# Windowed attention and a gated feed-forward on one core: 2 key tiles for every query tile from batch 2 on, output stores issued by ScalarE, another order of the first requests

## The chip, the core and the metric

The kernel runs on one core of a Trainium2 chip. The metric is the device time of one execution in microseconds (us), the median of several runs. TensorE (PE in the profile) multiplies; VectorE (DVE), ScalarE (ACT) and GpSimd (POOL) do elementwise work; SyncE (SP) only issues DMAs. ACT and POOL issue DMAs too.

## What is computed

The reference, cut to what matters:

```python
# q, k, v: (4, 8, 768, 64); n_sink = 4, window = 128; scale = 1/8
keep = (key < n_sink) | ((query - key >= 0) & (query - key < window))
a = softmax(where(keep, scale * q @ k.T, -1e9))
x = (a @ v)                       # -> (3072, 512), heads side by side
out = (relu(x @ w_gate) * (x @ w_val)) @ w_out     # d_ff = 1536
```

A query sees itself, the 127 keys ahead of it, and the first four keys of the sequence (the sinks).

## The kernel before

**Units and slots.** A unit is a pair of heads of one batch: 16 units, unit i is batch i // 4, pair i % 4. The order of all work is written out by hand in 96 slots. Slots 24b to 24b+23 hold the first feed-forward product of batch b: `chunk(b, g, m)` makes one tile of 128 hidden columns for half of the batch's 768 rows (g), four accumulating matmuls with w_gate and four with w_val (L362), a relu by ACT (L377) and a product by DVE (L379). After the chunk come the attention steps that `plan` lists for the slot, then from slot 24 on three matmuls of the second feed-forward product (`ffn2`, L404). Twelve of these make one output tile; ACT copies it out of PSUM (L408) and SP stores it (L409). `prep` lists what is issued ahead of a slot's chunk: loads, casts, transposes, copies.

**Attention of a unit** is spread over slots of the batch before. `Sg` computes scores for groups of key tiles (keys on partitions, L290; two matmuls a segment, one per head, on 64 rows each), exponentials by ACT (L298) and a product with a 0/1 mask by DVE (L300). `W` multiplies the exponentials by the values, 65 columns at a time (the 65th is ones, for the sum; L325), and DVE divides (L330, L331). Key tiles are 128 keys at the rows of `VROW`: even tiles start at 0, 244, 496, 748, odd tiles hold the four sinks and 124 keys. Because of this a query tile sometimes needs three key tiles. `SEG` lists the score segments of each group, `QSEG` which pieces each of the seven query tiles adds up: 10 segments and 16 pieces a head.

**Keys and queries on time.** For batches 2 and 3 the loads (`load_rows`, L161), the casts by POOL (`cast_rows`, L166), a store to DRAM in bfloat16 (`to_dram`, L171) and a transposing DMA into KQ (`turn`, L175) prepare a unit; POOL then copies the odd key tiles and the sinks in KQ (`odd_tiles`, L185 and L181), in the slot before the unit's first scores. Values are loaded by SP (`load_v`, L131) into one buffer `vf` and cast by POOL into `vn` (`cast_v`, L134): batch 2 loads in slots 23 to 29 and casts in 28 to 34, batch 3 loads in 44 to 50 and casts in 47 to 53.

**The way of the result.** For batches 2 and 3 a unit's normalised result goes by two SP stores to DRAM (`x_to_dram`, L151) in the slot after its `W`, and comes back by a transposing DMA two slots later into xT (`x_turn`, L155). Units 8 to 11 (batch 2) have their `W` in slots 35, 37, 39 and 41; the chunks of batch 2 begin at slot 48 and read all four quarters of xT.

**SP's queue is in order.** SP issues loads, stores and transposes as they are listed; an issue that must wait holds back all behind it. POOL's weight loads (L190) are in order with POOL's casts.

**Front.** Batch 0 is loaded in halves (`load_half`, L113: half c is pair c % 4, first or second 384 rows) and cast by POOL (`cast_half`, L118). SP requests the keys of halves 0 to 3, three value tiles, then halves 4 and 5; halves 6 and 7 and the other values wait for a write by DVE (L449). POOL's order is: cast of half 4, cast of half 5, weights of tiles 4 and 5; in slot 1 the cast of half 6, weights of tiles 6 and 7, the cast of half 7. Slot 6 holds the second half of W of units 0 and 1, which needs the other values.

Of the kernel before, what the change touches and what calls it, by code (L numbers as in the profile page):

```python
# [10 lines left out]
BF16 = mybir.dt.bfloat16  # L11
Alu = mybir.AluOpType
# [9 lines left out]
def kernel(  # L22
# [12 lines left out]
    nc = tc.nc  # L35
    B, H, S, D = q.shape
# [20 lines left out]
    KQ = [const.tile([128, 2 * S + 408], BF16, name=f"KQ{i}") for i in range(NT)]  # L57
    qT = [x[:, 0:S] for x in KQ]
    kE = [x[:, S:2 * S + 408] for x in KQ]
# [13 lines left out]
    msk = const.tile([128, 3, 512], BF16, name="msk")  # L73
    mb = const.tile([128, 2, 512], BF16, name="mb")
# [21 lines left out]
            [(4, 2, 128), (5, 2, 272)], [(5, 2, 396), (6, 2, 252), (4, 2, 416)]]  # L96

# [34 lines left out]

    def cast_v(b, j, rows=128, copy=nc.gpsimd.tensor_copy):
        copy(vn[b % 2][0:rows, j, :, 0:64], vf[0:rows, j, :, :])  # L134
# [10 lines left out]
    xd = [nc.dram_tensor(f"xd{i}", (1008, 128), BF16, kind="Internal").ap() for i in range(ND, B * NP)]  # L145

    def x_to_dram(u):

        x, d = xn[u.i % 2], xd[u.i - ND]
        for t, r0, n, i in ((0, 0, 128, 4), (1, 128, 124, 3)):  # L150
            nc.sync.dma_start(out=d[r0:r0 + 252 * i, :].rearrange("(i r) c -> r i c", r=252)[0:n, :, :],  # L151
                              in_=x[0:n, t:t + 2 * i - 1:2, :])

    def x_turn(u):
        nc.sync.dma_start(out=xT[u.b % 2][:, u.p, :], in_=xd[u.i - ND][8:8 + S, :], transpose=True)  # L155
        for x in range(2):
            ready[u.b, u.p, x] = True
# [78 lines left out]

    rot = [0]
# [41 lines left out]
    def Sg(u, s, ps=None):  # L279
        t, bias = u.i % NT, u.b == 0 and s in (0, 3)  # L280
        g, b0, n, segs = SEG[s]
        ps = ps or pair()
        at = [ps[h][:] if isinstance(ps, list) else ps[:, h, :] for h in range(2)]
        if bias:
            for h in range(2):
                nc.tensor.matmul(out=at[h][:, b0:n], lhsT=ident[:], rhs=mb[:, g, b0:n], start=True, stop=False,
                                 skip_group_check=True)
        for x0, q0, c0, c1 in segs:
            for h in range(2):
                nc.tensor.matmul(out=at[h][:, c0:c1], lhsT=kE[t][64 * h:64 * h + 64, x0:x0 + 128],  # L290
                                 rhs=qT[t][64 * h:64 * h + 64, q0:q0 + c1 - c0], start=not bias, stop=True,
                                 skip_group_check=True)
        x = ee[u.i % NE][:, g, :, b0:n]
        if isinstance(ps, list):
            for h in range(2):
                nc.scalar.activation(x[:, h, :], at[h][:, b0:n], Act.Exp, bias=0.0, scale=scale)
        else:
            nc.scalar.activation(x, ps[:, :, b0:n], Act.Exp, bias=0.0, scale=scale)  # L298
        if not bias:
            nc.vector.tensor_tensor(x, x, msk[:, g, b0:n].unsqueeze(1).to_broadcast([128, 2, n - b0]), op=Alu.mult)  # L300
# [9 lines left out]
    def W(u, part=None, bank=None):  # L310

        tiles = PART[part][0]
# [8 lines left out]
        for h in range(2):  # L321
            for t in tiles:
                c = 65 * (t - tiles[0])
                for i, (j, g, c0) in enumerate(QSEG[t]):
                    nc.tensor.matmul(out=at[h][:, c:c + 65], lhsT=ee[u.i % NE][:, g, h, c0:c0 + 128],  # L325
                                     rhs=vn[u.b % 2][:, j, 2 * u.p + h, 0:65],
                                     start=c == 0 and i == 0 and (bank is None or h == 0),
                                     stop=t == tiles[-1] and i == len(QSEG[t]) - 1, skip_group_check=True)
# [57 lines left out]
    def ffn2(b, t, m):  # L386
# [19 lines left out]
        if m == FM - 1:  # L406
            ot = outpool.tile([128, d_model], F32, name="ot")
            nc.scalar.copy(ot[:], op)  # L408
            nc.sync.dma_start(out=out[b * S + t * 128:b * S + (t + 1) * 128, :], in_=ot[:])  # L409

    with tc.manual_schedule():
# [6 lines left out]
        for c in (4, 5):  # L418
            load_half(c)
# [17 lines left out]
        for j in range(3):  # L437
            cast_v(0, j, copy=dve if j == 2 else nc.gpsimd.tensor_copy)
        load_w(2, 4)
        cast_half(4)  # L440
        cast_half(5)
        load_w(4, 6)
# [53 lines left out]
        prep[1] += [("half", 6), ("w", 6, 8), ("half", 7), ("setup3",), ("v", 0, 3), ("v", 0, 4), ("v", 0, 5), ("v", 0, 6)]  # L496
# [6 lines left out]
        for i, ts in ((8, (17, 20, 21, 24)), (9, (18, 21, 22, 26)), (10, (20, 23, 24, 28)), (11, (22, 24, 26, 30)),  # L503
# [4 lines left out]
            prep[at["S", i, 0] - 1].append(("sinks", i))  # L508
            prep[at["W", i, 0] + 1].append(("xd", i))
            prep[at["W", i, 0] + 3].append(("xturn", i))  # L510

        for b, s0, s1 in ((2, 23, 28), (3, 44, 47)):
            for j in range(7):
                prep[s0 + j].append(("lv", b, j))
                prep[s1 + j].append(("v", b, j))
# [3 lines left out]
        for s, (b, g, m) in enumerate(slots):  # L519
            for x in prep[s]:  # L520
# [27 lines left out]
                elif x[0] == "sinks":  # L548
                    odd_tiles(U[x[1]], nc.gpsimd.tensor_copy)
# [65 lines left out]
```

## Time and profile before

| What | Value |
|---|---|
| median of 3 runs | 251.91 us (251.41 to 252.01) |
| the profiled execution | 252.45 us |
| its span, from the first to the last instruction | 250.4 us |
| granted clock of TensorE | 1.0 |
| DMA | 40.07 MB in 75681 packets |
| output copies by ACT (L408) | 23, 0.59 us each |
| copies of odd key tiles by POOL (L185, L181) | 12 of 529 ns and 12 of 196 ns |
| casts of values by POOL (L134) | 27, 706 ns on average |
| value loads by SP (L131) | 52 issues, 0.30 to 4.5 us each |

The profile is of one execution. The span leaves out about 2 us around the instructions. In a row of a timeline the first number is the start in us from the span's start, the second the length; "x12" are twelve instructions merged. A matmul's end is modelled, so lengths of neighbours overlap and starts are to be compared. SPq is SP's queue: the length of a row is how long the issue took, not how long the transfer lasted. A landing mark is the moment when a DMA engine reports its share of a transfer as done; the trace has them for every DMA. In a row of the waits stand the engine and line that waited, for whom, the total in us, how often, and the longest.

### The profile page before, as it was taken

The page shows a single profiled execution, that of the slowest core. Times are in us where ns is not written, and L with a number is a line of the kernel's source. Part 1 is how long each engine was busy: PE and PEld are TensorE (multiplying, and loading weights), DVE is VectorE, ACT ScalarE, POOL GpSimd, SP SyncE. Part 2 cuts the span into 40 slices and gives each one's busy share as a digit, 9 for nine tenths or more (in the row PEclk, how much of TensorE's full clock was granted, in tenths as well). Part 3 has the DMA queues.
Part 4 walks back from the last instruction along what each step waited for, and adds up shares of the span by engine and source line. Part 5 has one row for each costly group of instructions (what it writes and reads, how often), then busy time and mean ns, then how long its engine had stood idle before and what let it go on. Part 6 is the DMA issues. An engine that isn't in the chain of part 4 may idle for free.

```text
span 250.4 us, 5321 instructions
## 1 busy us (share of the span) xinstructions
PE 238.6 (95%) x2084; PEld 139.9 (56%) x2084; DVE 116.6 (47%) x224; ACT 120.6 (48%) x220; POOL 69.7 (28%) x125
## 2 busy tenths in 40 slices
PE   7879969999999999999999999999999999999994
PEld 2456556655775555666555556565555555555443
DVE  5565854688662354687325546544322232222000
ACT  4849926999253455552336664532333323333111
POOL 7856664982633225631003600000000000000000
PEclk9999999999999999999999999999999999999999
DMA  6999999999989999899899311443211011110232
GB/s 207 251 211 259 245 338 235 213 164 219 337 274 231 242 184 323 278 230 210 211 227 229 82 42 39 106 106 77 75 44 42 0 42 46 43 42 1 86 126 84
DMA packets 75681, 40.07 MB, mean 160 GB/s; under 512 B 53512, under 2 KB 72712, under 8 KB 75656
## 3 DMA queue, kind: packets, MB, share of 16 engines
q1 hardware_dynamic: 67560, 34.10, 52.6%
q0 software_dynamic: 6864, 4.72, 12.7%
q10 hardware_dynamic: 1232, 0.92, 1.1%
q8 instruction: 16, 0.26, 0.4%
q14 instruction: 9, 0.07, 0.1%
HBM read 28.48 MB, written 11.25 MB: 159 GB/s over the span
## 4 chain that ended last, share of the span: by engine, by line
PE 70%; DMA 15%; SPq 6%; POOL 4%; issue 2%; ACT 1%; DVE 0%; POOLq 0%; DVEq 0%; ACTq 0%
PE g L362 38%; PE g L404 20%; SPq L131 5%; PE pp L325 4%; DMA vf<-in_v_dram 4%; DMA kf<-in_k_dram 4%; DMA wv<-in_moe_w_val_dram 3%; PE pp L404 3%; DMA qf<-in_q_dram 3%; PE pp L290 2%; POOL vn L134 1%; POOL ee L308 1%; SPq L113 1%; PE pp L398 1%; PE g L398 1%
## 5 line engine op out<-in xcount | busy, mean ns | idle before, releaser
L379 DVE TENSOR_TENSOR hT<-gs,g 128x384 bf16<-128x384 f32 (+2 forms) x96 | 53.0, 553 | 88.3 <-PE g L362 80.2
L377 ACT ACTIVATE gs<-g 128x384 f32<-128x384 f32 (+2 forms) x96 | 47.7, 497 | 77.0 <-PE g L362 75.9
L362 PE MATMUL g<-xT,wv 128*128 128x384 bf16 (+2 forms) x384 | 78.8, 326 | 2.7 <-DMA wv<-in_moe_w_val_dram 2.6
L362 PE MATMUL g<-xT,wg 128*128 128x384 bf16 (+2 forms) x384 | 78.8, 326 | 0.5 <-ACT xT L345 0.5
L404 PE MATMUL g<-wo,hT 128*128 128x512 bf16 x240 | 64.0, 379 | 0.3 <-ACT ot L408 0.2
L362 PEld LDWEIGHTS <-wv 128*128 128x128 bf16 x384 | 37.3, 98 | 29.1 <-DMA wv<-in_moe_w_val_dram 3.8
L362 PEld LDWEIGHTS <-wg 128*128 128x128 bf16 x384 | 36.2, 98 | 30.3
L298 ACT ACTIVATE ee<-pp 128x838 bf16<-128x838 f32 (+4 forms) x50 | 43.0, 904 | 9.5 <-PE pp L290 9.2
L404 PEld LDWEIGHTS <-hT 128*128 128x128 bf16 x276 | 25.5, 98 | 23.8 <-issue 0.7
L300 DVE TENSOR_TENSOR ee<-ee,msk 128x838 bf16<-128x838 bf16 (+3 forms) x44 | 32.2, 738 | 13.8 <-ACT ee L298 13.2
L134 POOL CAST vn<-vf 128x512 bf16<-128x512 f32 x27 | 18.6, 706 | 33.7 <-DMA vf<-in_v_dram 33.7
L325 PEld LDWEIGHTS <-ee 128*128 128x128 bf16 x512 | 18.1, 97 | 5.1 <-issue 3.2
L408 ACT COPY ot<-g 128x512 f32<-128x512 f32 x20 | 11.7, 587 | 17.5 <-PE g L404 17.5
L325 PE MATMUL pp<-vn,ee 128*128 128x65 bf16 x488 | 18.2, 193 | 1.4 <-POOL vn L134 1.3
L331 DVE TENSOR_TENSOR xn<-pp,rn 128x896 bf16<-128x896 f32 (+2 forms) x18 | 17.0, 943 | 0.6
L290 PEld LDWEIGHTS <-KQ 64*128 64x128 bf16 x328 | 10.9, 94 | 10.1 <-issue 8.2
L290 PE MATMUL pp<-KQ 64*128 64x3 bf16 (+5 forms) x316 | 15.8, 221 | 0.0
L166 POOL CAST kn<-kf 128x768 bf16<-128x768 f32 x12 | 10.2, 851 | 17.2 <-DMA kf<-in_k_dram 8.9
L166 POOL CAST qn<-qf 128x768 bf16<-128x768 f32 x12 | 11.3, 940 | 2.8 <-DMA qf<-in_q_dram 2.5
L185 POOL COPY KQ<-KQ 128x372 bf16<-128x372 bf16 x12 | 6.3, 529 | 11.5 <-DMA KQ<-kqd 6.8
L345 ACT COPY xT<-g 128x372 bf16<-128x372 bf16 (+2 forms) x10 | 5.4, 545 | 6.8 <-PE g L342 6.8
L404 PE MATMUL pp<-wo,hT 128*128 128x512 bf16 x36 | 8.1, 379 | 0.0
(80 smaller groups left out, 105.5 us busy)
## 6 DMA issues: line engine op xcount, KB each, us to landing
out_dram<-ot SPq DMA_DIRECT2D x23, 256.0 KB
kf<-in_k_dram SPq DMA_DIRECT2D x12, 384.0 KB
qf<-in_q_dram SPq DMA_DIRECT2D x12, 384.0 KB
vf<-in_v_dram SPq DMA_DIRECT2D x12, 256.0 KB
vf<-in_v_dram SPq DMA_DIRECT2D x12, 224.0 KB
kf<-in_k_dram SPq DMA_DIRECT2D x8, 192.0 KB
wo<-in_moe_w_out_dram POOLq DMA_DIRECT2D x3, 512.0 KB, 8.6
kqd<-qn SPq DMA_DIRECT2D x8, 192.0 KB
```

Of the source, the lines that this page charges most:

```text
L131: nc.sync.dma_start(out=vf[a0:a1, j, :, :], in_=v[b, :, s0:s0 + a1 - a0, :].rearrange("h s d -> s h d"))
L134: copy(vn[b % 2][0:rows, j, :, 0:64], vf[0:rows, j, :, :])
L166: nc.gpsimd.tensor_copy(dst[u.i % 2][:].rearrange("p (n h d) -> p h n d", n=NR, h=2), src[u.i % NQ][:].rearrange("p (h n d) -> p h n d", n ...
L290: nc.tensor.matmul(out=at[h][:, c0:c1], lhsT=kE[t][64 * h:64 * h + 64, x0:x0 + 128], rhs=qT[t][64 * h:64 * h + 64, q0:q0 + c1 - c0], start ...
L298: nc.scalar.activation(x, ps[:, :, b0:n], Act.Exp, bias=0.0, scale=scale)
L300: nc.vector.tensor_tensor(x, x, msk[:, g, b0:n].unsqueeze(1).to_broadcast([128, 2, n - b0]), op=Alu.mult)
L325: nc.tensor.matmul(out=at[h][:, c:c + 65], lhsT=ee[u.i % NE][:, g, h, c0:c0 + 128], rhs=vn[u.b % 2][:, j, 2 * u.p + h, 0:65], start=c == 0 ...
L331: nc.vector.tensor_tensor(x.rearrange("p t (h d) -> p h t d", h=2), o[:, :, :, 0:64], r.unsqueeze(3).to_broadcast([128, 2, n, 64]), op=Alu ...
L362: nc.tensor.matmul(out=ps[:, 0:n], lhsT=w[:, ko, m * 128:(m + 1) * 128], rhs=x[:, ko, c], start=ko == 0, stop=ko == KO - 1)
L377: nc.scalar.activation(gs[:, 0:n], gp[:, 0:n], Act.Relu, bias=0.0, scale=1.0)
L379: nc.vector.tensor_tensor(h[:, m, c], gs[:, 0:n], vp[:, 0:n], op=Alu.mult)
L404: nc.tensor.matmul(out=op, lhsT=hT[b % 2][:, m, t * 128:(t + 1) * 128], rhs=wo[:, m, :], start=m == 0, stop=m == FM - 1)
```

## The change

**Key tiles.** For batches 2 and 3 the query tiles are cut like the key tiles, at 0, 128, 256, 380, 504, 625, 746. A query tile t meets key tiles t-1 and t alone. What a tile of under 128 keys would miss is held twice: tiles 3 to 6 begin with copies of the 3 or 6 keys that lie ahead of the tile before them (`DUP`), beside the four sinks in tiles 2, 4 and 6 (`LEAD` counts both). New tables `SEG2`, `QSEG2` and masks `msk2` replace the old ones there: 7 segments and 13 pieces a head. KQ is 240 columns wider.

**Copies.** `key_tiles` replaces `odd_tiles` for these batches: six POOL copies a unit (3x4, 2x124, 2x3, 2x121, 2x6 and 22 columns), two slots ahead of the first scores and no longer one. The values are loaded to match (`load_v2`): batch 2 in slots 23, 25, 27, 28 with most tiles in two pieces (12 or 9 rows and 112), its casts in slots 27 to 33 and ahead of the slot's other steps; batch 3 in slots 38, 40, 42, 43 with tiles whole (124 or 121 rows), its casts unchanged. A unit's result goes to DRAM by four stores of 128, 124, 121 and 22 rows and no longer two of 128 and 124.

**Stores.** Output tiles of batches 0 to 2 are stored by ACT, directly behind its copy. Those of batch 3 stay with SP.

**Front.** Half 5 is requested after a write by DVE that follows DVE's cast of the third value tile. POOL asks for the weights of tiles 4 and 5 ahead of the cast of half 5, and for those of tiles 6 and 7 ahead of the cast of half 6.

**As built**, SP and ACT share eight semaphores for landings, taken in turn over both engines in program order, before the change and after it: each DMA waits until the eighth before it has landed.

The diff, cut (left out: the masks' setup and the choice between old and new tables in `Sg` and `W`):

```diff
+    K2 = [0, 128, 256, 380, 504, 625, 746, S]
+    LEAD = [0, 0, 4, 4, 7, 7, 10]
+    DUP = [None, None, None, (1, 3), (4, 3), (1, 6), (4, 6)]
+    PLACE = [0, 128] + [ODD + 128 * i for i in range(5)]
+    SEG2, QSEG2, at2 = {}, [[] for _ in range(7)], 0
+    for t in range(7):
+        if t % 2 == 0 and t < 6:
+            at2 = 0
+            SEG2[t // 2] = (t // 2, 0, 0, [])
+        g2 = min(t // 2, 2)
+        w = K2[min(t + 2, 7)] - K2[t]
+        SEG2[g2] = (g2, 0, at2 + w, SEG2[g2][3] + [(PLACE[t], K2[t], at2, at2 + w)])
+        QSEG2[t].append((t, g2, at2))
+        if t < 6:
+            QSEG2[t + 1].append((t, g2, at2 + K2[t + 1] - K2[t]))
+        at2 += w
...
+    def load_v2(b, x):
+
+        rows = lambda r0, r1: v[b, :, r0:r1, :].rearrange("h s d -> s h d")
+        if x == 0:
+            for t in (2, 4, 6):
+                nc.sync.dma_start(out=vf[0:4, t, :, :], in_=rows(0, 4))
+        for t in (2 * x, 2 * x + 1):
+            if t > 2:
+                if t > 6:
+                    continue
+                f, d = DUP[t]
+                nc.sync.dma_start(out=vf[f:f + d, t, :, :], in_=rows(K2[t - 1] - d, K2[t - 1]))
+            n, l = K2[t + 1] - K2[t], LEAD[t]
+            for a0, a1 in ((l, 16), (16, l + n)) if b == 2 and 0 < l and t < 6 else ((l, l + n),):
+                nc.sync.dma_start(out=vf[a0:a1, t, :, :], in_=rows(K2[t] + a0 - l, K2[t] + a1 - l))
...
-        for t, r0, n, i in ((0, 0, 128, 4), (1, 128, 124, 3)):
-            nc.sync.dma_start(out=d[r0:r0 + 252 * i, :].rearrange("(i r) c -> r i c", r=252)[0:n, :, :],
-                              in_=x[0:n, t:t + 2 * i - 1:2, :])
+        for t in range(0, 7, 2):
+            n, i = K2[t + 1] - K2[t], min(2, 7 - t)
+            nc.sync.dma_start(out=d[K2[t]:K2[t] + i * n, :].rearrange("(i r) c -> r i c", r=n), in_=x[0:n, t:t + i, :])
...
+    def key_tiles(u, copy):
+        e = kE[u.i % NT]
+        two = lambda c0, w: e[:, c0:c0 + 2 * w].rearrange("d (i c) -> d i c", c=w)
+        copy(e[:, ODD:ODD + 640].rearrange("d (i c) -> d i c", c=128)[:, 0:5:2, 0:4],
+             e[:, 0:4].unsqueeze(1).to_broadcast([128, 3, 4]))
+        for t in (2, 4):
+            n, l, d = K2[t + 1] - K2[t], LEAD[t], DUP[t + 1][1]
+            copy(two(PLACE[t], 128)[:, :, l:l + n], two(K2[t], n))
+
+            copy(two(PLACE[t + 1] + 1, 131)[:, :, 0:d], two(K2[t] - d, n)[:, :, 0:d])
+        copy(e[:, PLACE[6] + LEAD[6]:PLACE[6] + LEAD[6] + S - K2[6]], e[:, K2[6]:S])
...
-            nc.sync.dma_start(out=out[b * S + t * 128:b * S + (t + 1) * 128, :], in_=ot[:])
+            (nc.scalar if b < B - 1 else nc.sync).dma_start(out=out[b * S + t * 128:b * S + (t + 1) * 128, :], in_=ot[:])
...
-        for c in (4, 5):
-            load_half(c)
+        load_half(4)
...
+
+        nc.vector.memset(half(kf, 5)[0:1, 0:2], 0.0)
+        load_half(5)
         load_w(2, 4)
         cast_half(4)
+        load_w(4, 6)
         cast_half(5)
-        load_w(4, 6)
...
-        prep[1] += [("half", 6), ("w", 6, 8), ("half", 7), ("setup3",), ("v", 0, 3), ("v", 0, 4), ("v", 0, 5), ("v", 0, 6)]
+        prep[1] += [("w", 6, 8), ("half", 6), ("half", 7), ("setup3",), ("v", 0, 3), ("v", 0, 4), ("v", 0, 5), ("v", 0, 6)]
...
-            prep[at["S", i, 0] - 1].append(("sinks", i))
+            prep[at["S", i, 0] - 2].append(("sinks", i))
...
-        for b, s0, s1 in ((2, 23, 28), (3, 44, 47)):
+        for g2 in range(3):
+            prep[24 + g2].append(("setup4", g2))
+        prep[24].append(("setup5",))
+
+        for b, s0, s1 in ((2, 23, 27), (3, 38, 47)):
+            for j in range(4):
+                prep[s0 + 2 * j - j // 3].append(("lv2", b, j))
             for j in range(7):
-                prep[s0 + j].append(("lv", b, j))
-                prep[s1 + j].append(("v", b, j))
+                prep[s1 + j].insert(0 if b == 2 else len(prep[s1 + j]), ("v", b, j))
```

`setup4` (in slots 24 to 26) writes the masks by 20 DVE instructions on up to 256 columns each; `setup5` (slot 24) clears parts of KQ and of the exponentials by eight POOL instructions.

More of the change, by code (lines that the diff above doesn't have):

```diff
@@ L55 @@
     vn = [const.tile([128, 7, H, 66], BF16, name=f"vn{i}") for i in range(2)]
-    KQ = [const.tile([128, 2 * S + 408], BF16, name=f"KQ{i}") for i in range(NT)]
+    KQ = [const.tile([128, 2 * S + 648], BF16, name=f"KQ{i}") for i in range(NT)]
     qT = [x[:, 0:S] for x in KQ]
-    kE = [x[:, S:2 * S + 408] for x in KQ]
+    kE = [x[:, S:2 * S + 648] for x in KQ]
     ee = [const.tile([128, 3, 2, 640], BF16, name=f"ee{i}") for i in range(NE)]
@@ L73 @@
     msk = const.tile([128, 3, 512], BF16, name="msk")
+    msk2 = const.tile([128, 3, 512], BF16, name="msk2")
     mb = const.tile([128, 2, 512], BF16, name="mb")
@@ L142 @@
     kqd = [nc.dram_tensor(f"kqd{i}", (2 * S, 128), BF16, kind="Internal").ap() for i in range(ND, B * NP)]
-    xd = [nc.dram_tensor(f"xd{i}", (1008, 128), BF16, kind="Internal").ap() for i in range(ND, B * NP)]
+    xd = [nc.dram_tensor(f"xd{i}", (S, 128), BF16, kind="Internal").ap() for i in range(ND, B * NP)]
     def x_to_dram(u):
         x, d = xn[u.i % 2], xd[u.i - ND]
-        for t, r0, n, i in ((0, 0, 128, 4), (1, 128, 124, 3)):
-            nc.sync.dma_start(out=d[r0:r0 + 252 * i, :].rearrange("(i r) c -> r i c", r=252)[0:n, :, :],
-                              in_=x[0:n, t:t + 2 * i - 1:2, :])
+        for t in range(0, 7, 2):
+            n, i = K2[t + 1] - K2[t], min(2, 7 - t)
+            nc.sync.dma_start(out=d[K2[t]:K2[t] + i * n, :].rearrange("(i r) c -> r i c", r=n), in_=x[0:n, t:t + i, :])
     def x_turn(u):
-        nc.sync.dma_start(out=xT[u.b % 2][:, u.p, :], in_=xd[u.i - ND][8:8 + S, :], transpose=True)
+        nc.sync.dma_start(out=xT[u.b % 2][:, u.p, :], in_=xd[u.i - ND], transpose=True)
         for x in range(2):
@@ L235, in setup2, with setup4, setup5 @@
             cp(msk[:, 2, 252:272], band[:, 0:20])
+    def setup4(g):
+        cp, ms = nc.vector.tensor_copy, nc.vector.memset
+        for t, (_, _, c0, c1) in zip(range(2 * g, 7), SEG2[g][3]):
+            l = LEAD[t]
+            cp(msk2[:, g, c0:c1], band[:, l:l + c1 - c0])
+            if DUP[t]:
+                f, d = DUP[t]
+                ms(msk2[0:l, g, c0:c1], 0.0)
+                nc.vector.tensor_scalar(msk2[0:l, g, c0:c0 + d], band[0:l, f - 1:f - 1 + d], -1.0, 1.0,
+                                        op0=Alu.mult, op1=Alu.add)
+            if t in (2, 4, 6):
+                ms(msk2[0:4, g, c0:c1], 1.0)
+        if g == 0:
+            ms(msk2[0:4, 0, 0:256], 1.0)
+    def setup5():
+        for i in range(NT):
+            nc.gpsimd.memset(kE[i][:, PLACE[6] + 32:PLACE[6] + 128], 0.0)
+        for i in range(NE):
+            nc.gpsimd.memset(ee[i][:, 2, :, 404:514], 1.0)
     rot = [0]
@@ L280, in Sg @@
         t, bias = u.i % NT, u.b == 0 and s in (0, 3)
-        g, b0, n, segs = SEG[s]
+        g, b0, n, segs = (SEG if u.b < 2 else SEG2)[s]
+        mask = msk if u.b < 2 else msk2
         ps = ps or pair()
@@ L299, in Sg @@
         if not bias:
-            nc.vector.tensor_tensor(x, x, msk[:, g, b0:n].unsqueeze(1).to_broadcast([128, 2, n - b0]), op=Alu.mult)
+            nc.vector.tensor_tensor(x, x, mask[:, g, b0:n].unsqueeze(1).to_broadcast([128, 2, n - b0]), op=Alu.mult)
     ready = {}
@@ L310, in W @@
     def W(u, part=None, bank=None):
-        tiles = PART[part][0]
+        tiles, seg = PART[part][0], QSEG if u.b < 2 else QSEG2
         n, w = len(tiles), 65 * len(tiles)
@@ L323, in W @@
                 c = 65 * (t - tiles[0])
-                for i, (j, g, c0) in enumerate(QSEG[t]):
+                for i, (j, g, c0) in enumerate(seg[t]):
                     nc.tensor.matmul(out=at[h][:, c:c + 65], lhsT=ee[u.i % NE][:, g, h, c0:c0 + 128],
@@ L327, in W @@
                                      start=c == 0 and i == 0 and (bank is None or h == 0),
-                                     stop=t == tiles[-1] and i == len(QSEG[t]) - 1, skip_group_check=True)
+                                     stop=t == tiles[-1] and i == len(seg[t]) - 1, skip_group_check=True)
         x, r = xn[u.i % 2][:, tiles[0]:tiles[0] + n, :], rn[u.i % 2][:, :, 0:n]
@@ L548 @@
                 elif x[0] == "sinks":
-                    odd_tiles(U[x[1]], nc.gpsimd.tensor_copy)
+                    key_tiles(U[x[1]], nc.gpsimd.tensor_copy)
+                elif x[0] == "setup4":
+                    setup4(x[1])
+                elif x[0] == "setup5":
+                    setup5()
+                elif x[0] == "lv2":
+                    load_v2(*x[1:])
                 elif x[0] == "lv":
```

## The prediction

> **What bounds the kernel now.** I read the busy shares and the slices first, then TensorE's timeline, the waits, and SyncE's timeline in the stretch where batch 2's activations are prepared.
>
> ```profile
> PE 238.6 (95%) x2084; PEld 139.9 (56%) x2084; DVE 116.6 (47%) x224; ACT 120.6 (48%) x220; POOL 69.7 (28%) x125
> PE   7879969999999999999999999999999999999994
> DMA  6999999999989999899899311443211011110232
> ```
>
> TensorE (PE) has work from slice 6 to the end; outside the first 42 us it loses almost nothing. So a removed matmul shortens the run, as long as nothing becomes late. The DMA engines are full up to slice 22 (137 us): there the margin is thin.
>
> TensorE's timeline, two slots (start, length, instruction group):
>
> ```profile
> 82.60 0.81 PE L362 MATMUL g<-xT,wv 128*128 128x384 bf16 x4
> 83.25 0.81 PE L404 MATMUL g<-wo,hT 128*128 128x512 bf16 x3
> 83.90 0.81 PE L362 MATMUL g<-xT,wg 128*128 128x384 bf16 x4
> 84.55 0.81 PE L362 MATMUL g<-xT,wv 128*128 128x384 bf16 x4
> 85.29 0.63 PE L290 MATMUL pp<-KQ 64*128 64x244 bf16 x12
> 85.85 0.82 PE L404 MATMUL g<-wo,hT 128*128 128x512 bf16 x3
> ```
>
> Lengths overlap (the end is modelled); starts count. Eight chunk matmuls of 384 columns take 83.90 to 85.20, 0.423 ns a column. The 12 score matmuls (six pairs, one of each pair per head) take 0.56 us for 1006 columns: 0.43 for columns, and (0.56-0.43)/6 = 22 ns more a pair.
>
> ```profile
> PE pp L325 <- POOL vn L134: 1.3, 2, 0.9
> PE g L362 <- DMA wv<-in_moe_w_val_dram: 2.6, 2, 1.7
> ```
>
> From the waits (total, times, longest): TensorE stands once 0.9 us for batch 2's values (slot 35, at 99.5), and in front 2.6 us for weights.
>
> SyncE's queue (SPq), the stretch that decides:
>
> ```profile
> 106.65 1.32 SPq L155 DMA_TRANSPOSE xT<-xd  x1
> 108.92 0.84 SPq L151 DMA_DIRECT2D xd<-xn  x2
> 109.80 2.77 SPq L175 DMA_TRANSPOSE KQ<-kqd  x1
> 112.67 0.54 SPq L409 DMA_DIRECT2D out_dram<-ot  x1
> ...
> 122.24 0.97 SPq L151 DMA_DIRECT2D xd<-xn  x2
> 123.27 0.60 SPq L409 DMA_DIRECT2D out_dram<-ot  x1
> 123.92 2.38 SPq L175 DMA_TRANSPOSE KQ<-kqd  x1
> 126.41 1.21 SPq L155 DMA_TRANSPOSE xT<-xd  x1
> 127.67 0.58 SPq L131 DMA_DIRECT2D vf<-in_v_dram  x1
> ```
>
> From 108.92 on one issue follows the other without a gap. The last transpose of batch 2 (unit 11) goes out at 126.41; its last landing mark in the trace is at 129.16. Slot 48, batch 2's first chunk, starts at 130.08 and reads that quarter of xT with its fourth matmul, at 130.6. The margin is 1.4 us.
>
> **What the Trainium skill says.** "DMA: Bandwidth & Descriptors", section "Why a DMA increments its semaphore by 16 and not by 1": a copy is spread over the largest number of engines up to 16 that divides its slowest dimension on both sides. The trace agrees: copies of 128 and 112 rows leave 16 landing marks, the store of 124 rows 5 (four engines, and one mark for the rest). Uncontended, that store (372 rows of 256 B) took 153.18 to 156.24, 3.06 us; its neighbour with 512 on 16 engines 1.98. Section "Queues, rings and completion order" of the same page: SP and ACT each have one ring on every one of the same 16 engines, consumed in order. The trace agrees: from 115.9 to 140 SP's DMAs land in order of issue, at most 1.7 us apart. Section "Issuing engines are not separate DMA queues": another issuer saves only the issuing time. On ACT the four qf loads cost 0.49 us each; no run shows a store there in mid-kernel. "TensorE: Matmul & The Clock Gate", section "Back-to-back issue gap", gives about 81 ns a matmul at 128 columns; the trace differs: 32 value matmuls of 65 columns take 105.98 to 106.94, 30 ns each. I use the trace.
>
> **Part 1: fewer key tiles (batches 2, 3).** A unit's score pairs fall from 10 to 7 and its columns per head from 1425 to 1408: 3 x 22 + 17 x 0.423 = 73 ns. Value matmuls fall from 32 to 26: 6 x 30 = 180 ns. For 8 units 2.0 us, 1.0 in each batch. The ends: 1.4 (values alone), 2.5 (a pair at 40 ns, if the 0.1 us gap ahead of L290 shrinks too). All of it lies on TensorE's path. Exponentials and mask products keep their sizes within 1.2%. The 20 mask instructions in slots 24 to 26 cost VectorE some 3.3 us (0.06 to 0.27 each, from the like rows at 16.8 to 18.3); it idles 1.39 in each such slot, 4.2 in all, and a product may slip by 1 us, which the third g bank covers. If that cover is gone: up to 1 us.
>
> **Part 2: values and key copies.** Batch 2's value casts come ahead of the other GpSimd work of their slots and no longer behind the cast at 96.85, so the 0.92 us wait in slot 35 goes. Six key copies replace two: two small ones and two of 242 to 248 columns more, about 1.65 us for 0.73 (from the 529 and 196 ns rows). GpSimd is 28% busy. The tightest is unit 11: its copies wait behind the cast of unit 13's queries, end near 107.1, and are wanted in slot 38 at 107.7. Late next would be these; a stall here costs nothing extra if slot 48 has to wait anyway.
>
> **Part 3: stores by ACT.** 18 stores leave SP (0.33 to 0.86 each) and cost ACT 0.4 to 0.5 after an output copy every fourth slot. Queued behind is the next relu. ACT has 1.46 us idle in plain slots, and a relu may be 1.1 us late before its bank is wanted (slot 51: done at 139.1, bank wanted at 140.2). I cost this at nothing. But SP and ACT share eight landing semaphores in turn, and as built each DMA waits until the eighth before it has landed. So SP now waits for ACT: the query load of unit 13 (issued at 94.46 now) waits for the store of slot 34, copied at 97.75 to 98.34, landed near 101 (2.0 us as at 138.73, to 5 us as at 98.37). ACT's own waits are covered: slot 42's store needs a DMA landed near 114 and goes at 119.6, slot 46's one landed near 120.5 and goes at 127.
>
> **Part 4: the SP queue up to unit 11's transpose.** PE reaches slot 37 about 1.3 us earlier (0.92 + 0.4), so unit 9's result could be stored from 107.6. (a) The wait for slot 34's store moves the loads after it to 101.1 to 102.5, unit 12's store to 102.6, unit 8's to 103.5, and through their landings unit 9's to about 110.0. (b) From there to the transpose SP now needs 126.41-108.92 = 17.5. Added are 14 loads of batch 3's values, moved from behind this transpose to slots 38 to 43, ahead of it: 14 x 0.45 = 6.3; and two more row stores for each of units 9, 10, 11: 6 x 0.45 = 2.7. Two out stores leave: -1.2. Sum 7.8. (c) New waits: the transpose of unit 13's keys waits for slot 42's store (SP there at 120.4, landed 122.3: 1.9), and a load of 3 rows waits for the second load of 124 rows. That one puts 124 x 8 = 992 pieces on four engines, 248 each; the 93 each of the present store take 1.1 to 1.7 us between landings, so 3.0 to 4.5 us a load, twice: 2.2 more. Part overlaps (b): I take 2.0 of 0 to 4.1. (d) A drained ring makes the key transposes' issues shorter (1.6 to 2.8 now): -1.0 of -1.5 to 0. The transpose goes at 110.0+17.5+7.8+2.0-1.0 = 136.3 and lands 2.75 later, 139.05. Slot 48 wants it at 130.6-0.92-1.0 = 128.65. TensorE, in order, stands 10.4 us.
>
> **Part 5: front.** The second query and key half of unit 1 waits for a VectorE write at 12.7, and weights 4 to 8 are asked for up to 4 us sooner. This takes away up to 0.9 us at 17.8 and 1.7 at 32.8. But slot 6 then waits for values that now land at 33.06 and 33.34, behind the same total of bytes in slices where DMA is full; their casts end at 34.4, where TensorE is now. I take 0; the ends are -0.7 and +0.7.
>
> **The sum.** +10.4 - 0.92 - 2.0 = +7.5 on the profiled execution's 252.45 (span 250.4 and 2 around it): 259.95. That execution is 0.54 above the median of the runs, 251.91; on it: 259.4. With (a) and (c) at nothing and (d) at -1.5 the transpose lands at 134.15 and the time is 254.5; with (c) full, (d) nothing and 1.5 more behind the value loads in the rings, about 264.
>
> **Rivals.** *SP keeps up* (the other side): freed of stores, SP sends the transposes early enough. Place: slot 48; price 0; it decides if unit 11's transpose lands before 128.65. Then 251.91-2.0-0.92 = 249.0. For it: SP idles 99.7 to 102.6 today, and the value loads wait for nobody in batch 3 until slot 56. Against it: the gapless issue from 108.92 and a margin of 1.4. *Key copies late, transposes in time*: unit 11's copies miss slot 38 by 1 to 3 us: 250.5 to 252. Against it: one cause drives both. *ACT held*: if SP falls 7 us behind before slot 46, ACT's store blocks relus too; that adds to the forecast, 264 or more. The shares: the program does what the words say in all of them.
>
> **The numbers.** Forecast (254.5 to 264) 0.73; slower but below that 0.06; same, through late key copies, 0.05; SP keeps up 0.13; over 264 0.03. Within 0.3% (0.75 us) is about what a measurement here can't tell from no change. Faster 0.13, same 0.05, slower 0.82. The range 251.5 to 264.5 leaves out most of the two faster cases and the top.
>
> **What will show it.** Right: in slot 48 one idle stretch of TensorE of 5 to 15 us ended by the DMA of xT, an xT transpose issued near 136, value matmuls in batch 2 and 3 at 26 a unit, no wait for vn in slot 35. Wrong: xT landed before the chunk asks, or TensorE idle at slots 29 to 38 instead, or the front shorter by over 1 us.

## The result, and the profile after

The changed kernel takes 270.86 us (median of 4 runs, 268.82 to 273.41) beside 251.96 for the kernel before on the same chip: 1.073 times as long, 95% interval 1.067 to 1.079. One of the four runs (273.41) fell into a slower state: medians here and below are of all runs except one of 1360 us that e2_late had, ratios and intervals of the undisturbed runs alone. The forecast was 259.4. The sign and the place were right; the stall is 1.7 times as long as forecast, and the time lies above the top of the range.

The slices of the changed kernel (forty of 6.7 us; busy tenths of TensorE, its granted clock in tenths, busy tenths of the DMA engines):

```profile
PE 238.7 (89%) x1967; PEld 138.4 (51%) x1988; DVE 120.2 (45%) x244; ACT 121.0 (45%) x220; POOL 77.7 (29%) x165
PE   7987789999999999999300999999999999999994
PEclk9999979999999999999955799999999999999999
DMA  7999999999799876979568310233411111001222
```

TensorE is as long busy as before (238.6), with 117 recorded matmuls fewer (96 in the program; 21 of L479 are missing from the trace), and now stands for nearly three slices. Two things are easily missed: its clock falls to a half in and behind the hole, and from the fourteenth slice on the DMA engines are full in few slices only; in the hole they are busy three to eight tenths. What holds TensorE is not a lack of bandwidth.

The hole in TensorE's timeline (start, length, group; in brackets the idle before it and what ended it), and its row in the waits:

```profile
129.59 0.49 PE L437 MATMUL g<-xT,wg 128*128 128x384 bf16 x2
139.94 0.48 PE L437 MATMUL g<-xT,wg 128*128 128x384 bf16 x1 [9.87 <-DMA xT<-xd]
148.26 0.48 PE L437 MATMUL g<-xT,wg 128*128 128x384 bf16 x1 [7.84 <-DMA xT<-xd]
148.53 1.48 PE L437 MATMUL g<-xT,wv 128*128 128x384 bf16 x4
149.95 1.02 PE L365 MATMUL pp<-KQ 64*128 64x256 bf16 x8
150.90 1.14 PE L479 MATMUL g<-wo,hT 128*128 128x512 bf16 x3
151.88 0.81 PE L437 MATMUL g<-xT,wg 128*128 128x384 bf16 x4
```

```profile
PE g L437 <- DMA xT<-xd: 17.7, 2, 9.9
```

This is slot 48: two matmuls run on the xT of units 8 and 9, the third waits 9.87 us for unit 10's, the fourth 7.84 us for unit 11's. The forecast had one wait of 10.4; that unit 10 would be late too was not in it. From 148.26 to 151.88 the matmuls take nearly twice their time: the four w_val matmuls of the chunk last from 148.53 to the scores' start at 149.95, 1.42 us; in the kernel before the same stretch is 0.74:

```profile
130.73 0.81 PE L362 MATMUL g<-xT,wv 128*128 128x384 bf16 x4
131.47 0.63 PE L290 MATMUL pp<-KQ 64*128 64x244 bf16 x12
```

SyncE's queue ahead of the two transposes (the length is that of the issue):

```profile
125.87 1.32 SPq L213 DMA_TRANSPOSE KQ<-kqd  x1
127.24 0.47 SPq L169 DMA_DIRECT2D vf<-in_v_dram  x1
127.75 3.78 SPq L166 DMA_DIRECT2D vf<-in_v_dram  x1
131.58 0.28 SPq L169 DMA_DIRECT2D vf<-in_v_dram  x1
131.96 4.21 SPq L209 DMA_DIRECT2D kqd<-qn  x1
136.22 0.43 SPq L209 DMA_DIRECT2D kqd<-kn  x1
136.69 1.19 SPq L193 DMA_TRANSPOSE xT<-xd  x1
...
145.48 1.15 SPq L193 DMA_TRANSPOSE xT<-xd  x1
```

In the kernel before the same two transposes went at 120.95 and 126.41. The rows at 127.24 and 131.58 are batch 3's value loads of 124 rows; their last landing marks are at 134.29 and 138.09, 7.1 and 6.5 us after the start of their issue. The issue right behind each, a load of three rows and a store, takes 3.78 and 4.21 us where such issues elsewhere in this queue take 0.3 to 0.8. From 127.2 to 136.2 SyncE gets four DMAs out. ScalarE issues an output store in 0.34 us in the same time (at 128.46), so it is SyncE's own issuing that is held.

### The profile page after: what moved, and what is told of

Its sections match the earlier page's. It is cut to its first block, busy times and chain, and to the rows that moved or that the text cites. A ratio compares the mean times of both kernels' runs of the same rounds, so it can differ in the third digit from the quotient of the medians.

```text
span 268.8 us, 5201 instructions
## 1 busy us (share of the span) xinstructions
PE 238.7 (89%) x1967; PEld 138.4 (51%) x1988; DVE 120.2 (45%) x244; ACT 121.0 (45%) x220; POOL 77.7 (29%) x165
## 3 DMA queue, kind: packets, MB, share of 16 engines
q0 software_dynamic: 6864, 4.72, 12.0%
## 4 chain that ended last, share of the span: by engine, by line
PE 73%; DMA 10%; SPq 9%; DVE 3%; issue 2%; ACT 1%; POOL 0%; ACTq 0%; DVEq 0%; POOLq 0%
PE g L437 42%; PE g L479 18%; PE pp L400 5%; DMA qf<-in_q_dram 5%; DMA vf<-in_v_dram 4%; PE pp L365 4%; PE pp L479 3%; SPq L153 2%; SPq L166 2%; SPq L209 2%; SPq L213 1%; DMA xT<-xd 1%; DVE msk L292 1%; PE g L417 1%; SPq L190 1%
## 5 line engine op out<-in xcount | busy, mean ns | idle before, releaser
L437 PE MATMUL g<-xT,wg 128*128 128x384 bf16 (+2 forms) x384 | 79.9, 328 | 18.5 <-DMA xT<-xd 17.7
L437 PE MATMUL g<-xT,wv 128*128 128x384 bf16 (+2 forms) x384 | 80.1, 330 | 0.0
L479 PE MATMUL g<-wo,hT 128*128 128x512 bf16 x219 | 60.9, 381 | 1.5 <-issue 0.3
L437 PEld LDWEIGHTS <-wg 128*128 128x128 bf16 x384 | 36.2, 98 | 40.9 <-issue 10.8
L373 ACT ACTIVATE ee<-pp 128x838 bf16<-128x838 f32 (+7 forms) x50 | 42.7, 899 | 8.1 <-PE pp L365 7.6
L479 PEld LDWEIGHTS <-hT 128*128 128x128 bf16 x276 | 25.5, 98 | 25.1 <-issue 2.8
L375 DVE TENSOR_TENSOR ee<-ee,msk 128x838 bf16<-128x838 bf16 (+6 forms) x44 | 32.0, 730 | 13.9 <-ACT ee L373 13.3
L400 PEld LDWEIGHTS <-ee 128*128 128x128 bf16 x464 | 17.0, 99 | 5.0 <-issue 3.1
L400 PE MATMUL pp<-vn,ee 128*128 128x65 bf16 x440 | 17.0, 195 | 2.1 <-POOL vn L172 2.1
L365 PE MATMUL pp<-KQ 64*128 64x3 bf16 (+11 forms) x268 | 15.8, 236 | 0.0
L365 PEld LDWEIGHTS <-KQ 64*128 64x128 bf16 x280 | 9.9, 95 | 10.4 <-issue 7.6
L204 POOL CAST qn<-qf 128x768 bf16<-128x768 f32 x12 | 10.8, 900 | 7.4 <-DMA qf<-in_q_dram 7.4
L479 PE MATMUL pp<-wo,hT 128*128 128x512 bf16 x36 | 8.1, 379 | 0.0
L229 POOL COPY KQ<-KQ 128x12 bf16<-128x12 bf16 x8 | 1.9, 236 | 18.7 <-DMA KQ<-kqd 11.0
```

Source lines behind the costliest of these rows:

```text
L204: nc.gpsimd.tensor_copy(dst[u.i % 2][:].rearrange("p (n h d) -> p h n d", n=NR, h=2), src[u.i % NQ][:].rearrange("p (h n d) -> p h n d", n ...
L375: nc.vector.tensor_tensor(x, x, mask[:, g, b0:n].unsqueeze(1).to_broadcast([128, 2, n - b0]), op=Alu.mult)
L437: nc.tensor.matmul(out=ps[:, 0:n], lhsT=w[:, ko, m * 128:(m + 1) * 128], rhs=x[:, ko, c], start=ko == 0, stop=ko == KO - 1)
L479: nc.tensor.matmul(out=op, lhsT=hT[b % 2][:, m, t * 128:(t + 1) * 128], rhs=wo[:, m, :], start=m == 0, stop=m == FM - 1)
```

## The experiments

After the traces my theory was this (N below): the narrow loads of batch 3 block SyncE's queue, and the rest of the forecast stands. Its rivals are the place and number of the loads (P), the stores on ScalarE through the shared landing semaphores (S), values that come too late (V) and the front (F).

Times are medians, ratios are to the kernel before, run beside it on the same chip, with 95% intervals. "Issued" and "landed" are of unit 11's xT transpose, in the profiled execution; "stall" is TensorE's idle for xT in slot 48 there.

| Kernel | us | Ratio | Issued | Landed | Stall |
|---|---|---|---|---|---|
| before | 251.96 | 1 | 126.41 | 129.16 | 0 |
| changed | 270.86 | 1.073 (1.067-1.079) | 145.48 | 148.22 | 17.7 |
| e1_split | 266.51 | 1.054 (1.047-1.061) | 139.02 | 141.83 | 12.3 |
| e3_spstores | 265.91 | 1.051 (1.044-1.058) | 139.29 | 142.45 | 12.2 |
| e9_split_sp | 260.10 | 1.032 (1.026-1.037) | 135.31 | 138.12 | 7.8 |
| e2_late | 257.95 | 1.022 (1.013-1.031) | - | - | - |
| e7_late_again | 256.62 | one run | 129.00 | 133.22 | 3.4 |
| e8_late_sp | 253.86 | 1.004 (0.999-1.008) | 128.42 | 131.74 | 0 |
| e10_best | 249.83 | 0.986 (0.981-0.991) | 126.87 | 129.65 | 0 |
| e11_early | 261.76 | 1.033 (1.026-1.041) | 135.64 | 138.87 | 6.8 |
| e12_early_narrow | 268.56 | 1.063 (1.055-1.070) | 138.11 | 144.12 | 12.7 |
| e13_twostores | 268.62 | 1.063 (1.058-1.068) | 142.14 | 145.15 | 16.3 |

Beside the experiments the kernel before took 252.35 to 253.06 us, on three chips. Differences in us between two rows are therefore good to about 1 us: by the ratios e1_split, e3_spstores and e9_split_sp gain 4.8, 5.6 and 10.4 us where the medians below give 4.4, 5.0 and 10.8.

**The narrow loads** are batch 3's two value loads of 124 rows, on four DMA engines each. e1_split, on the changed kernel:

```diff
-            for a0, a1 in ((l, 16), (16, l + n)) if b == 2 and 0 < l and t < 6 else ((l, l + n),):
+            for a0, a1 in ((l, 16), (16, l + n)) if 0 < l and t < 6 else ((l, l + n),):
```

> The changed kernel with one edit: batch 3's 124-row value loads are split into 12 and 112 rows, as batch 2's are. Theory N (the narrow loads block SyncE's queue): in the changed kernel they land on four engines, and the two DMA issues behind them take 3.8 and 4.2 us instead of some 0.5, so SyncE stands for some 7 us. Split, the loads land on sixteen engines, no issue near 127 to 137 us takes over 1.5 us, unit 10's xT transpose is issued near 131 instead of 136.7 and unit 11's near 138 instead of 145.5; the idle of TensorE in slot 48 falls from 17.7 us to between 6 and 10, and the time from 270.9 to between 259 and 264. Theory P (it is the place and the number of the loads, not their width): the split adds two issues, the idle stays at 16 to 19 us, and the time at 270 to 273.

SyncE's queue in e1_split:

```profile
126.19 0.95 SPq L169 DMA_DIRECT2D vf<-in_v_dram  x2
127.18 0.58 SPq L166 DMA_DIRECT2D vf<-in_v_dram  x1
127.80 0.71 SPq L169 DMA_DIRECT2D vf<-in_v_dram  x2
128.61 0.79 SPq L209 DMA_DIRECT2D kqd<-qn  x1
...
129.91 1.41 SPq L193 DMA_TRANSPOSE xT<-xd  x1
```

The two long issues are gone, though there are two DMAs more: unit 10's transpose goes at 129.91 instead of 136.69. So narrow loads hold the queue. (Behind this transpose the edit splits the two loads of 121 rows as well.) But the stall falls only to 12.3, not below 10, and 266.51 us is over the 259 to 264 expected: theory N has the mechanism, and something besides it.

**Behind the transposes.** e2_late, on the changed kernel:

```diff
-        for b, s0, s1 in ((2, 23, 27), (3, 38, 47)):
+        for b, s0, s1 in ((2, 23, 27), (3, 44, 47)):
```

> The changed kernel with one edit: batch 3's value loads are listed from slot 44 on, behind unit 11's xT transpose, instead of from slot 38; their width stays. Theories N and P: nothing of the loads lies ahead of the two xT transposes; these are issued near 124 and 129 us instead of 136.7 and 145.5, the idle in slot 48 falls below 2 us, and the time comes to between 251 and 254 (270.9 less 17.7, and less up to 2 for the time in which TensorE ran slower after the idle). Rival theory S (the shared landing semaphores of SyncE and ScalarE hold the queue, with stores on ScalarE, whatever the value loads do): the xT transpose of unit 11 is still issued after 134, an idle of 6 us or more stays, and the time is over 258. Rival theory V (the values come too late for slot 56): an idle of TensorE in slot 56, ended by a POOL copy of vn, of 2 us or more.

257.95 us, from three executions, is over the 251 to 254 of theory N. The trace is of the fourth, of 1360 us, and says nothing here; so the kernel ran once more.

> The kernel e2_late once more, for its trace: it measured 258 us, where 251 to 254 was expected. Theory S: the idle in slot 48 is still 4 us or more, ended by a DMA of xT, though no value load lies ahead of it. Theory V: the idle in slot 48 is under 2 us, and 3 us or more of idle stand in slot 56, ended by a POOL copy of vn. Theory F (the front): neither, and the slots up to 24 end 3 us or more later than in the kernel before (74.2 us).

Nearest to theory S, a little under its mark of 4: 3.4 us of stall with no value load ahead. Behind it TensorE ran at half speed from 133.3 to 138.9 (granted clock 0.50), which costs half of that, some 2.8 us, besides. The loads are still narrow there (4.52 us of issue behind one, at 136.12), but nothing that slot 48 needs is queued behind them any more.

**The stores.** e3_spstores, on the changed kernel:

```diff
-            (nc.scalar if b < B - 1 else nc.sync).dma_start(...)
+            nc.sync.dma_start(...)
```

> The changed kernel with one edit: all output stores are issued by SyncE again. Theory N: the value loads hold the queue as before and SyncE has the stores of batches 0 to 2 to issue besides, but the wait of unit 13's load for a store goes (6.4 us at 95 to 102 us); most of this wait had been made up by 125 us; the idle in slot 48 is 14 to 20 us and the time 268 to 274. Theory S: with the stores off ScalarE the shared landing semaphores no longer tie the two queues; the idle falls by 6 us or more, and the time to 265 or below.

Here theory N fell, as far as it gave the stores nothing: they are worth 5.0 us, as much as the narrow loads, and the stall falls by 5.5 (theory S had 6 or more, and 265 us or below: nearly met). The first place where the traces part is this, the changed kernel first, e3_spstores below:

```profile
95.01 0.46 SPq L199 DMA_DIRECT2D kf<-in_k_dram  x1
101.93 0.37 SPq L199 DMA_DIRECT2D qf<-in_q_dram  x1
...
111.49 1.52 SPq L193 DMA_TRANSPOSE xT<-xd  x1
```

```profile
95.77 0.47 SPq L199 DMA_DIRECT2D qf<-in_q_dram  x1
99.60 0.36 SPq L484 DMA_DIRECT2D out_dram<-ot  x1
...
106.43 1.59 SPq L193 DMA_TRANSPOSE xT<-xd  x1
```

SyncE waits because of the same store in both, near 100: in the one until ScalarE's store has landed (101.91), in the other until the tile can be stored. But with the store in its own queue the wait stands behind the key and query loads of units 13 and 14, which are issued by 95.77 and landed at 102.61. With the store on ScalarE and a shared landing semaphore the wait stands ahead of unit 13's query load: three big loads go at 101.93 to 103.56 and land at 105.58 to 109.50, directly ahead of unit 8's attention output, which lands at 111.41 instead of 105.72. The transpose that needs it, 5 us later, holds all behind it.

e6_actstores is the kernel before with the store line of the changed kernel.

> The kernel before with one edit: stores of batches 0 to 2 are issued by ScalarE. Theory N: without the early value loads the xT transposes of units 10 and 11 stay ahead of their use (they landed at 123.7 and 129.2 us, wanted at 130.1), so an added wait of some 2 us on SyncE costs little; no idle over 1 us in slot 48, and the time is 251 to 254. Theory S: the shared landing semaphores hold SyncE's queue by 4 us or more at 95 to 125 us, unit 11's transpose lands after 132, and the time is 255 or more.

254.48 us, ratio 1.005 (1.002 to 1.008), a stall of 0.9 us in slot 48: near theory N. On this stretch SyncE waits 0.5 us in all for stores of ScalarE, where the changed kernel has one wait of 6.4. What such stores cost depends on which DMA falls on the same semaphore. Is it the one wait of 6.4 us? e13_twostores, on the changed kernel:

```diff
-            (nc.scalar if b < B - 1 else nc.sync).dma_start(...)
+            (nc.scalar if b < B - 1 and (b, t) not in ((0, 1), (0, 2)) else nc.sync).dma_start(...)
```

> The changed kernel with one edit: the second and third output store of batch 0 (near 91 and 99 us) are issued by SyncE, all others of batches 0 to 2 by ScalarE. In the built program no load of units 12 to 14 then waits for a store of ScalarE. Theory S1 (what the stores on ScalarE cost is the one wait of 6.4 us, which puts four loads behind it into the way of unit 8's attention output): unit 8's xT transpose is issued near 106.5 us instead of 111.5, as with all stores on SyncE, and the time falls by 4 to 6 us, to 265 to 267. Theory S2 (it is the sum of waits for stores, at 112, 121 and 128 us too): under half of the gain, 268.5 to 271.

Unit 8's transpose goes at 105.02, as theory S1 has it. The time falls by 2.2 us only. In e13_twostores SyncE runs into the next store, landed at 114.79: behind the key transpose issued at 109.06 nothing goes out until 114.81, 4.4 us of wait where the changed kernel, being later, found none. Theory S2 on the time: it is a chain of waits, and taking the first away uncovers the next.

**Both.** e8_late_sp has the edits of e2_late and e3_spstores, e9_split_sp those of e1_split and e3_spstores.

> The changed kernel with two edits: batch 3's value loads behind unit 11's xT transpose, and all stores on SyncE. Theory N with S (value loads ahead and the stores on ScalarE each hold SyncE's queue, some 5 us each): no idle over 1 us in slot 48, 251 to 254 us. Theory D (the number of DMAs is too much for SyncE's queue, wherever these two lie): an idle of 3 us or more stays in slot 48, 256 or more. Theory V: 3 us or more of idle in slot 56, 255 or more.

> The changed kernel with two edits: batch 3's 124-row loads split into 12 and 112 rows, and all stores on SyncE; the loads stay in slots 38 to 43. Alone the first gave 4.4 us and the second 5.0. If the two act apart, the idle in slot 48 falls from 17.7 to some 7 us and the time to 259 to 263. If both gave the same time (the queue drained once), it stays at 264 to 267. If nothing but the two held the queue, there is no idle and the time is 251 to 254.

e8_late_sp has no stall in slot 48, 253.86 us. The stores are only a part of this in the traces: unit 11's xT lands 1.5 us earlier than in e7_late_again, and slot 48 begins 1.75 us later (131.00 for 129.25). The times say more: 253.86 us, of twelve runs, for the 257.95 of e2_late, of three. Theory V was there too, smaller and in slot 54: 2.1 us of idle at 146.8, ended by a key copy of POOL that stood behind a cast of values landed at 147.16; TensorE then ran at half speed from 149.9 to 153.3. In e9_split_sp the two add up: -4.4 and -5.0 alone, -10.8 together. The 7.8 us of stall left are the place and number of the loads: e10_best below differs from e9_split_sp in their place and in the front, and has no stall.

**The loads alone, in the kernel before.** e11_early moves batch 3's loads, split as they are, from slot 44 to 38 (the same one-number edit as e2_late, the other way). e12_early_narrow besides:

```diff
-        parts = [(0, 4, 0), (4, 16, VROW[j] + 4), (16, 128, VROW[j] + 16)] if j in (1, 3, 5) else ...
+        parts = ... if j in (1, 3, 5) and b < 3 else [(0, 4, 0), (4, 128, VROW[j] + 4)] if j in (1, 3, 5) else ...
```

> The kernel before with one edit: batch 3's value loads from slot 38 on instead of 44; they stay split (12 and 112 rows). 12 DMA issues come ahead of unit 11's xT transpose. At 0.45 us each they are worth 5.4 us: unit 11's xT lands near 134.6 us instead of 129.2, wanted at 130.1: an idle of 3.5 to 5.5 us in slot 48, and 255 to 258. If the count of issues costs nothing (the queue has slack): under 1 us of idle and 251 to 253.5.

> As e11_early, but batch 3's loads of 124 rows are not split: three issues fewer, three loads on four engines. Theory N (a narrow load holds SyncE's queue for 3 to 4 us at an issue behind it): unit 11's xT lands near 140 to 144, the idle in slot 48 is 9 to 14 us, the time 261 to 267, more than e11_early by 5 or more. Theory P (only count and place matter): 1.4 us less than e11_early.

e11_early first, e12_early_narrow below, at unit 9's transpose:

```profile
116.66 1.14 SPq L131 DMA_DIRECT2D vf<-in_v_dram  x3
117.84 2.41 SPq L155 DMA_TRANSPOSE xT<-xd  x1
```

```profile
116.06 1.02 SPq L131 DMA_DIRECT2D vf<-in_v_dram  x2
117.12 4.72 SPq L155 DMA_TRANSPOSE xT<-xd  x1
```

Twelve split loads move unit 11's transpose by 9.2 us, not by 5.4, and the stall is 6.8, over what was expected. In that execution unit 9's store already goes 1.0 later than before (109.93 for 108.92); what is left is 0.68 us a load, and the transposes of units 9 and 10 behind such loads take 2.4 and 2.3 us to issue instead of 1.2. Three DMAs fewer, but narrow, cost 6.8 us more, and 268.56 us is over the 261 to 267 of theory N: P alone is excluded, N and P both have a share.

**The front.** e4_front is the kernel before with the changed kernel's front, e5_oldfront the changed kernel with the old one.

```diff
-        for c in (4, 5):
-            load_half(c)
+        load_half(4)
...
+        nc.vector.memset(half(kf, 5)[0:1, 0:2], 0.0)
+        load_half(5)
         load_w(2, 4)
         cast_half(4)
-        cast_half(5)
         load_w(4, 6)
+        cast_half(5)
...
```

> The kernel before with one edit: the front's order of the changed kernel (the load of half 5 behind a gate after the first casts of values, the weights ahead of the casts of halves 5 and 6). Theory F: the front's new order costs 1.2 us by itself (slot 24 began at 75.4 us in the changed kernel and at 74.2 in the one before): ratio 1.003 to 1.008. Theory F0: it costs nothing by itself, the 1.2 us of the changed kernel's trace being of that execution's clock (0.7 in the fifth slice of forty): ratio 0.998 to 1.002.

> The changed kernel with the front in the order of the kernel before. If the front's 1.0 us (e4_front) passes through to the end: 268.5 to 270.2. If the SyncE queue alone sets the stall and swallows the front: 270.5 to 271.5.

e4_front: 253.30 us, ratio 1.004 (1.002 to 1.006), 1.0 us: theory F. e5_oldfront: 270.13 us, ratio 1.061 (1.051 to 1.070), 0.7 us below the changed kernel, both with a spread of over 4 us: in the expected direction, and not told apart. One trace is a poor witness here: slot 24 begins between 73.7 and 75.2 us in the seven traces with the old front, and between 73.8 and 76.1 in the eight with the new one.

**Four stores of attention output.** e14_fourstores, on the kernel before:

```diff
-        for t, r0, n, i in ((0, 0, 128, 4), (1, 128, 124, 3)):
+        for t, r0, n, i in ((0, 0, 128, 2), (4, 504, 128, 2), (1, 128, 124, 2), (5, 632, 124, 1)):
```

> The kernel before with one edit: each unit's output of attention goes to DRAM in four DMAs instead of two (two tiles each, from batch 2 on). Six more issues lie ahead of unit 11's xT transpose. If they cost the 0.45 us each that the prediction took: 2.7 us, less the 0.9 of slack, so an idle of 1.5 to 2.1 us in slot 48 and a ratio of 1.006 to 1.009. If they cost nothing, because the KQ transposes behind them are issued the sooner: ratio 0.998 to 1.003.

253.40 us, ratio 1.004 (1.002 to 1.007), between the two. The trace shows no stall. Unit 11's transpose goes at 126.62, 0.2 later than before, but unit 9's store had gone 0.8 earlier (108.09 for 108.92): the way between them takes 18.5 us for 17.5. So the six stores cost some 1.0 us there, not 2.7; the key transposes behind them are issued in 1.3 to 2.2 us instead of 2.2 to 2.8. Without a stall this does not explain the 1.0 us of the median, which stays open.

**What is left of the change.** e10_best: the edits of e1_split, e2_late, e3_spstores and e5_oldfront together.

> The changed kernel with four edits: batch 3's value loads behind unit 11's xT transpose, split into 12 and 112 rows, all stores on SyncE, and the front in the order of the kernel before. What is left of the change are the two key tiles for each query tile, the paired copies, and batch 2's earlier values. In e8_late_sp 2.1 us were lost to a key copy that stood on POOL behind a cast of late values, and the front costs 1.0 us in e4_front; split, the values should land before their casts. If the 2.9 us of parts 1 and 2 of the prediction are there: 248.5 to 250.5 us, ratio 0.985 to 0.995. If the fewer matmuls give nothing, or POOL is still held: ratio 0.997 to 1.006.

249.83 us, ratio 0.986 (0.981 to 0.991): faster than both kernels. From slot 24 to the end its trace takes 174.3 us, the kernel before 176.2. It could be up to 1.0 better; from VectorE's and POOL's timelines of e10_best:

```profile
77.24 2.15 DVE L292 COPY msk<-band 128x248 bf16<-128x248 bf16 x1
```

```profile
77.88 0.53 POOL L306 MEMSET KQ<- 128x96 bf16 x4
78.36 0.96 POOL L309 MEMSET ee<- 128x220 bf16 x4
```

A mask copy of 248 columns takes 2.15 us, the next, of 245, 0.27 (at 79.69). The long one ends at 79.39; a cast by POOL and its eight fills run from 77.11 to 79.3. The Trainium skill's page "SBUF — State Buffer", section "Who interferes with whom", says that a VectorE copy in a two-port mode and a GpSimd instruction exclude each other for a whole instruction. These rows agree with that, and go further: the copy ends only after nine GpSimd instructions in a row. In the changed kernel the copy of 248 columns takes 0.22 us, and the one of 245, which there lies beside the same nine, 1.96. The products behind it slip, and TensorE waits once for one of them, 1.03 us at 83.2. No run moved the fills; that they cause it is read from the rows of two kernels, not tested.

## Why the prediction was right in its mechanism and wrong in its size

The path was the one forecast: SyncE's queue, unit 11's transpose, a stall in slot 48. Two terms of the sum failed, (c) and (a), and one was missing, the clock after the stall. On the profiled executions' spans the forecast was +7.5 us and the measurement +18.4 (250.4 to 268.8). The 10.9 between them, term by term:

| Term | Forecast | Measured |
|---|---|---|
| (a) unit 9's store at | 110.0 | 113.05 |
| (b) and (d), issues added on the way from there to unit 11's transpose (measured: what the other terms leave) | 6.8 | 7.8 |
| (c) waits on that way | 2.0 | 7.1 |
| unit 11's transpose issued | 136.3 | 145.48 |
| from issue to landing | 2.75 | 2.74 |
| slot 48 wants it (its landing less the stall) | 128.65 | 130.5 |
| stall | 10.4 | 17.7 |
| slow matmuls after the stall | 0 | 2.0 |
| front (slot 24 at 75.40, before 74.16) | 0 | 1.24 |
| parts 1 and 2 | -2.92 | -2.5 |

The last row is -1.73 from slot 24 to slot 48 (54.19 us for 55.92) and -0.79 from slot 49 to the end (116.92 for 117.71). Slot 48 wants its xT later than forecast mostly by the front and by what parts 1 and 2 fell short.

- **Term (c) failed.** "a load of 3 rows waits for the second load of 124 rows ... twice: 2.2 more ... I take 2.0 of 0 to 4.1". The loads themselves were costed well (3.0 to 4.5 us each; from 134.29 to 138.09, 3.8). What was wrong is where that time goes: I let SyncE wait once, at a semaphore eight DMAs later, and took it that in the meantime issuing goes on. It does not. The very next issue lasts about as long as one such load takes the engines: 3.78 + 4.21, less 0.9 for two ordinary issues, 7.1 where the forecast had 2.0. In e1_split unit 10's transpose goes 6.8 us earlier (1.0 of it won ahead of the loads) and the time is 4.4 less; e12_early_narrow costs 6.8 in time. Why an issue lasts so long no run shows.
- **Term (a) had the mechanism and a quarter of the size**: +1.1 on the 108.92 of the kernel before, where +4.1 came. "The wait for slot 34's store moves the loads after it to 101.1 to 102.5" is what happened (101.93 to 103.56), and "through their landings unit 9's to about 110.0" is how it went; unit 9's store was at 113.05. The loads' landings delay unit 8's output by 5.7 us, and its transpose waits for that. Part 3's "I cost this at nothing" holds for ScalarE, for which TensorE waits no longer than before; in all the stores cost 5.0 us.
- **Terms (b) and (d) hold** as a sum (7.8 for 6.8), and roughly in their parts: by the lengths of their issues the 14 loads, without the long wait, take some 6 us, the stores of output 3.5 more than before, the key transposes 0.4 less. Such prices do not carry over: in the kernel before, six added stores cost 1.0 (e14_fourstores), not 2.7, and a load 0.68 (e11_early), not 0.45.
- **After the stall.** This was not in the sum. Slot 48 takes 22.3 us; without its 17.7 of idle 4.6, where the kernel before needs 2.6. "TensorE: Matmul & The Clock Gate", section "Part 1: The HAM clock gate", says that an idle window of about 3.4 us halves the clock, and that it takes at least about as long a busy one to get it back. The trace agrees: the granted clock is 0.50 from 134.5, 4 us into the idle, to 151.6, 3.3 us into the work. It lasted longer elsewhere, 5.6 us of work in e7_late_again and 6.2 in e11_early; and in e8_late_sp 2.1 us of idle were enough, less than the page's figure. There the measurement decides. I had the page and a stall of 10 us, and did not put them together.
- **Part 5, front.** Forecast 0, ends -0.7 and +0.7. e4_front: +1.0 (0.4 to 1.6). In the changed kernel's trace the 1.24 is not lost where part 5 looked: slot 6's values are in use at 34.30, as said (34.43 before). Behind these waits TensorE ran at half speed from 35.5 to 39.0, worth some 1.7 us; the trace of the kernel before has no such stretch. e4_front's trace has none either: it loses 0.45 us up to there and 0.6 to batch 1's values near 64. How the front costs its 1.0 us is open.
- **Parts 1 and 2 were right.** Value matmuls come 26 to a unit in 0.95 us for 1.13, the wait in slot 35 is gone, unit 11's copies hold nobody. (The 81 ns a matmul that the prediction sets aside are for 128 columns, the 30 ns that it takes are for 65. At 128 columns seven transposing matmuls, L342, start 56 ns apart in the kernel before, 73.12 to 73.51, so the trace differs there too.) In e10_best 1.9 us are there in the end, and 1.0 more are taken by the masks, for which part 1 named the cover and its price.
- **The rivals.** "SP keeps up" was excluded by the trace, and "Key copies late" too. "ACT held" did not come: slot 46's store goes at 128.46, for the 127 forecast. The range's top had (c) at 4.1 and 1.5 for the rings; it had no end for a queue that stops issuing.

## What to carry to other kernels

Cost a DMA by the pieces that each of its engines gets before costing it by its bytes. A load with 248 pieces on each of four engines held the issue of whatever came next, while the stores of 2 x 124 rows, 62 pieces on each of four, did not (the next issue took 0.5 to 0.9 us). Such a load belongs behind everything urgent, or split. Moving stores to another issuer need not free the first one if both draw on the same completion semaphores: look up in the built program who waits for whom. And a stall of TensorE can cost more than its length, here from 2.1 us of idle on.

## What the runs showed of the hardware

- A value load of 124 rows on four engines (992 pieces) lands 3.7 to 3.8 us after the one before it (changed kernel, e3_spstores, e7_late_again), and the issue right behind it on SyncE takes 3.2 to 4.7 us, whatever it is: a load of three rows (3.78), a store (4.21), an xT transpose (4.72). It is the issue itself that lasts; the semaphore that e12_early_narrow's transpose takes had been free since 113.48, before its issue at 117.12.
- A key transpose right behind a 124-row store of attention output takes 2.2 to 2.8 us to issue (kernel before); with a 121-row and a 22-row store between them 1.4 (e8_late_sp), but 2.7 once in the changed kernel (at 115.39). This may be the same effect, smaller; no run was made for it.
- Behind 17.7 us of idle TensorE ran at half speed for 3.3 us, which cost 2.0. Elsewhere it was 5.6 us behind 3.4 of idle (e7_late_again), 6.2 behind 6.8 (e11_early), 3.2 behind 7.8 (e9_split_sp) and, after 0.9 us at full speed, 3.4 behind 2.1 (e8_late_sp). Half of these stretches, 1.6 to 3.1 us, is my estimate of what each cost.
- SyncE stood 6.4 us (95.5 to 101.9) ahead of a load because the DMA eighth before it, a store issued by ScalarE, had not landed; with that wait gone it stood 4.4 us for the next such store (e13_twostores).
